# Exchanging the halves of a key tile's partitions: a permutation on TensorE and copies by ScalarE, or two DMAs

## The chip, the cores and the metric

One core of one Trainium2 chip runs the whole program. The metric is device time in microseconds (us), the median of several executions. One more execution, profiled, gives the trace.

## What is computed

Decayed causal attention over 4 batches of 8 heads (576 positions of 64 numbers), then a mixture of experts that sends each token to one of 8 experts, then a dense feed-forward layer. The change lies in the attention.

```python
scores = scale * np.matmul(q, k.transpose(0, 1, 3, 2))
decay = cum[:, :, :, None] - cum[:, :, None, :]
scores = np.where(causal, -1e9, scores + decay)
attn = np.exp(scores - max);  attn = attn / (sum(attn) + 1e-9)
attn_out = np.matmul(attn, v)
x = _moe_ref(attn_out as [2304, 512], ...)
return _moe2_ref(x, ...)
```

## The kernel before

Every number is held as two 16-bit parts, a high and a low one, so that TensorE can work in 16 bits. After the turn of queries and keys by DMA, a tile `xy[hb][:, i, 0, h]` has the high parts of a query block's 64 dimensions on partitions 0 to 63 and the low parts on 64 to 127, and `xy[hb][:, i, 1, h]` has the same of the keys. One product of the two gives high times high plus low times low. For the crossed terms the kernel needs the keys once more, with the two halves of the partitions exchanged: that is the tile `yw[hb]` (five blocks `i` of four heads, 128 columns each). `scores` (lines 568 to 608) multiplies each query block by both.

The work is cut into 8 half batches `hb` of four heads. `hb` 0 is prepared in its own way (`prep_first`, not touched). For `hb` 1 to 7, `prep_load` fetches, `prep` splits into parts, `prep_turn` (line 318) turns by DMA in three pieces, and `prep_swap` makes `yw`.

The attention is a loop over 96 units (two heads and a set of query blocks each; 12 units to a half batch, 6 to a pair of heads), as a software pipeline written out by hand: the program order is the order on every engine. Step n does `scores` of unit n+2 (TensorE), `parts_hi` of unit n-1 (ScalarE, line 671, reads `pt`), `parts_lo` of n-1 (VectorE, lines 678 and 682, reads `pt`), `maxima` of n+2 (VectorE, line 627), `values` of n-3 (TensorE, lines 713 and 727), `exps` of n+1 (ScalarE, line 650) and `turn` of n (TensorE, line 662, writes `pt`; every sixth unit writes a second tile `ptb`, line 666). Then come the side jobs that a table of numbers `PRM` gives to that step by `at(step, function)`: loads, splits, stores, routing, and in later steps parts of the first expert. The tiles `pt` and `ptb` share a pool of three PSUM slots, `ps_pt`, and a slot comes free when `parts_lo` has read it.

The half batch `hb` begins at unit 12*hb, whose scores stand in step 12*hb-2. Its swap stands in step 12*hb-6, -6, -5, -5, -6, -6 and -7 (`hb` 1 to 7; the last number of the table's rows `hb1` to `hb7`). It is two DMAs of 64 partitions each, issued by SyncE, whose queue holds all loads, turns and stores in program order.

Of the kernel before, what the change touches and what calls it, by code (L numbers as in the profile page):

```python
# [10 lines left out]
F32 = mybir.dt.float32  # L11
F16 = mybir.dt.float16
# [4 lines left out]
AF = mybir.ActivationFunctionType  # L17
# [74 lines left out]
def kernel(  # L92
# [17 lines left out]
    nc = tc.nc  # L110
# [4 lines left out]
    P = 128  # L115
    NT = 5
# [17 lines left out]
    const = ctx.enter_context(tc.tile_pool(name="const", bufs=1))  # L134
# [9 lines left out]
    identf = const.tile([P, P], F32, name="identf")  # L144
    identb = const.tile([P, P], BF16, name="identb")
    identh = const.tile([P, P], F16, name="identh")
    maskb = const.tile([P, P], BF16, name="maskb")
    mask4 = const.tile([P, 64], BF16, name="mask4")
    one3 = const.tile([P, P], BF16, name="one3")
# [34 lines left out]
    ps_pt = mid.enter_context(tc.tile_pool(name="ps_pt", bufs=3, space=PSUM))  # L184
# [66 lines left out]
    xy = {}  # L251
    yw = {}
# [93 lines left out]
            else:  # L346
                nc.vector.tensor_copy(yw[0][:, 2 * i + a, :, 0:n], tp[:, :, 0:n])

    def prep_swap(hb, part=None):

        if part in (0, None):
            yw_ = ywp.tile([P, NT, 4, P], F16, tag="yw", name="yw")
            yw[hb] = yw_
        c = (slice(0, 4), slice(4, 5), slice(0, NT))[2 if part is None else part]
        for g in range(2):
            src = slice(64 - 64 * g, 128 - 64 * g)
            dst = slice(64 * g, 64 * g + 64)
            nc.sync.dma_start(out=yw[hb][dst, c], in_=xy[hb][src, c, 1])

    def blank(hb):  # L360

# [37 lines left out]
    def identities():  # L399
        make_identity(nc, identf)  # L400
        nc.gpsimd.memset(maskb, 0.0)
        mh = maskb.rearrange("p (a c) -> p a c", a=2)
        nc.gpsimd.affine_select(
            out=mh, in_=mh, pattern=[[-1, 2], [-2, 64]], base=0, channel_multiplier=1,
            compare_op=ALU.is_ge, fill=-8.0e9,
        )

        nc.gpsimd.memset(one3, 0.0)
        nc.gpsimd.memset(one3[0:3], 1.0)
        nc.gpsimd.memset(cbt[0], 0.0)  # L410
        nc.gpsimd.memset(mask4, 0.0)
        nc.gpsimd.affine_select(
            out=mask4, in_=mask4, pattern=[[-1, 64]], base=0, channel_multiplier=1,
            compare_op=ALU.is_ge, fill=-8.0e9,
        )
# [13 lines left out]
    def cum_log():  # L429
        fs = cum["fs"]  # L430
        nc.vector.tensor_scalar(out=fs, in0=fs, scalar1=1e-4, scalar2=1.0, op0=ALU.max, op1=ALU.min)
        nc.scalar.activation(out=fs, in_=fs, func=AF.Ln)

        nc.scalar.activation(out=cum["one"][:, 0:1], in_=cum["one"][:, 0:1], func=AF.Exp, scale=0.0)
# [481 lines left out]
    def at(step, fn, *args):  # L916
        side.setdefault(max(step, -2), []).append((fn, args))
# [3 lines left out]
    for hb in range(1, 2 * B):  # L921
        o = PRM["hb" + str(hb)]
        s0 = 12 * hb
        for i in range(3):
            at(s0 + o[i], prep_load, hb, i)
            at(s0 + o[3 + i], prep, hb, i)
            at(s0 + o[6 + i], prep_turn, hb, i)
        if hb < 3:
            at(s0 + o[3], blank, hb)
        at(s0 + o[9], prep_swap, hb)  # L930
    for b in range(B):
        o = PRM["v" + str(b)]
        for t in range(NT):
# [3 lines left out]
    for gp in range(B * NPAIR):  # L937
        o = PRM["gp" + str(gp)]
# [8 lines left out]
    for b in range(B - 1):  # L947
        o = PRM["rt" + str(b)]
# [26 lines left out]
    o = PRM["tb"]  # L975
# [304 lines left out]
    o = PRM["e"]  # L1280
# [4 lines left out]
    for s in range(NE):  # L1285
        m1e, m2e = wsel(s)
        o = PRM["es" + str(s)]
# [8 lines left out]
    o = PRM["a"]  # L1296
# [15 lines left out]
    prep_load(0, 2)  # L1312
    identities()
    nc.vector.tensor_copy(identh, identf)
    nc.vector.tensor_copy(identb, identf)
    cum_log()
    prep_hi(0, 0)
# [17 lines left out]
    o = PRM["st"]  # L1335
# [228 lines left out]
    with tc.If(more > 0):  # L1564
# [3 lines left out]
        for e in range(E):  # L1568
# [7 lines left out]
            out=inb, in0=jr, in1=sx[:, :, 0:1].rearrange("p e o -> p o e").to_broadcast([P, 32, E]), op=ALU.is_ge  # L1576
        )
        nc.vector.tensor_tensor(
            out=inb2, in0=jr, in1=sx[:, :, 1:2].rearrange("p e o -> p o e").to_broadcast([P, 32, E]), op=ALU.is_ge
# [11 lines left out]
            out=ro, in0=ro, in1=sx[:, :, 0:1].rearrange("p e o -> p o e"), op=ALU.subtract  # L1591
# [19 lines left out]
        for c in (1, 2):  # L1611
            nc.vector.scalar_tensor_tensor(
                out=off[:, 0, :], in0=sel[:, c, :], scalar=noff[:, c - 1:c], in1=off[:, 0, :], op0=ALU.mult, op1=ALU.add
# [4 lines left out]
            out=inb2, in0=inb2, scalar=float(P), in1=off.to_broadcast([P, 32, E]), op0=ALU.mult, op1=ALU.add  # L1618
# [167 lines left out]
```

## Time and profile before

| | |
|---|---|
| median of 3 runs | 914.95 us (914.14 to 916.05) |
| the profiled execution | 907.73 us, of which its span is 905.6 us |
| granted TensorE clock over the span | 0.957 |
| busy: TensorE, VectorE, ScalarE, GpSimd | 88%, 56%, 35%, 32% of the span |
| attention | about 18 to 300 us of the span |
| first turn (line 662) of unit 0, of unit 95 | 24.31 us, 292.98 us |

A stretch in which every engine is partly idle is read by its waits: an engine works in program order, so whatever its next instruction waits for holds all that stands behind it. In the rows below a time at the start of a line is counted from the start of the span; a bracket at the end gives the idle time ahead of that instruction and what ended it. PE is TensorE, PEld its weight load, DVE VectorE, ACT ScalarE, POOL GpSimd, SPq the queue of SyncE.

### The profile page before, as it was taken

The numbers are of one execution on the slowest core, as the hardware profiler recorded it, in microseconds if no ns is written. First come the engines' busy times: TensorE is split into PE (matmuls) and PEld (weight loads), VectorE is DVE, ScalarE is ACT, GpSimd is POOL, SyncE is SP. The second block draws the span as 40 slices with busy tenths as digits, with TensorE's granted clock in tenths as the row PEclk, the third lists the DMA queues.
The fourth block names the chain that finished last, engine by engine and source line by source line (L and its number), as shares of the span: only waits on it lengthen the run. The fifth ranks groups of instructions, "written<-read, shape, count | busy, mean of one in ns | idle before, by whom it ended". The sixth has DMA issues, their size and how long they took to land. (4 is left out here: it accounts for less than half of the span.)

```text
span 905.6 us, 15603 instructions
## 1 busy us (share of the span) xinstructions
PE 796.8 (88%) x5565; PEld 446.1 (49%) x5565; DVE 511.5 (56%) x1244; ACT 320.6 (35%) x630; POOL 291.5 (32%) x347
## 2 busy tenths in 40 slices
PE   3987767678988885989998899999999999999995
PEld 2776656555766332434443484444444444444442
DVE  6887868686785354669788589970025015303400
ACT  4777648666665122523333122220012002101200
POOL 4443344343435224513221144350024114312400
PEclk9899998888998996999999999999999999999998
DMA  6889999989952898999999371300002000000000
GB/s 148 159 145 175 159 125 190 178 202 169 154 80 61 138 149 182 266 247 229 249 261 230 68 188 47 93 1 24 24 24 47 23 24 1 1 24 23 1 24 23
DMA packets 226631, 103.16 MB, mean 114 GB/s; under 512 B 192843, under 2 KB 213944, under 8 KB 226554
## 3 DMA queue, kind: packets, MB, share of 16 engines
q1 hardware_dynamic: 221018, 87.29, 51.5%
q0 software_dynamic: 5536, 14.86, 4.9%
q8 instruction: 46, 0.75, 0.4%
q14 instruction: 31, 0.25, 0.1%
HBM read 49.06 MB, written 15.59 MB: 71 GB/s over the span
## 5 line engine op out<-in xcount | busy, mean ns | idle before, releaser
L1675 PE MATMUL a<-x,wi 128*128 128x512 f16 x768 | 166.9, 379 | 2.7 <-DVE t L1683 2.7
L1680 DVE TENSOR_SCALAR t<-a,al 128x512 f32<-128x512 f32 (+1 forms) x80 | 55.5, 694 | 194.3 <-PE a L1675 192.7
L1675 PEld LDWEIGHTS <-wi 128*128 128x128 f16 x960 | 93.8, 98 | 99.2 <-issue 7.0
L1701 PEld LDWEIGHTS <-g 128*128 128x128 f16 x864 | 84.5, 98 | 101.9
L1691 POOL TENSOR_TENSOR g<-t,g 128x512 f16<-128x512 f32 (+1 forms) x80 | 86.2, 1078 | 111.8 <-ACT g L1690 110.1
L1231 PE MATMUL y<-wcc,ht 128*128 (+1 forms) x456 | 107.5, 391 | 12.6 <-DMA ht<-hs 12.4
L1196 PE MATMUL h<-wcc,xgt 128*128 (+1 forms) x456 | 105.6, 387 | 6.5 <-DMA xgt<-xg 6.2
L1690 ACT ACTIVATE g<-t 128x512 f16<-128x512 f32 (+1 forms) x80 | 46.7, 586 | 148.0 <-DVE t L1683 141.7
L1701 PE MATMUL o<-wo,g 128*128 128x512 f16 x432 | 96.2, 379 | 0.0
L1701 PE MATMUL o<-wob,g 128*128 128x512 f16 x432 | 96.2, 379 | 0.0
L662 PE MATMUL pt<-identf,t 128*128 128x128 f32 x384 | 66.1, 298 | 31.0 <-DVE p L678 15.4
L650 ACT ACTIVATE t<-e,nm 128x512 f32<-128x512 f32 (+2 forms) x144 | 81.3, 602 | 18.0 <-DVE e L627 12.8
L1231 PEld LDWEIGHTS <-ht 128*128 128x128 f16 x480 | 47.6, 100 | 72.1 <-DMA ht<-hs 14.6
L1196 PEld LDWEIGHTS <-xgt 128*128 128x128 f16 x480 | 47.3, 99 | 63.8 <-DMA xgt<-xg 6.8
L678 DVE SCALAR_TENSOR_TENSOR p<-pt,p 128x512 f16<-128x512 f32 x96 | 65.5, 683 | 22.3 <-ACT p L671 21.8
L1706 ACT ACTIVATE ob<-o 128x512 f32<-128x512 f32 x18 | 10.7, 597 | 169.3 <-PE o L1701 169.3
L1708 POOL DMA_INDIRECT out_dram<-ob,tka x18 | 17.6, 976 | 162.5 <-ACT ob L1706 162.5
L627 DVE TENSOR_SCALAR_CACHE_REDUCE e<-s 128x512 f32<-128x512 f32 (+3 forms) x128 | 58.1, 481 | 9.9 <-PE s L580 9.9
L662 PEld LDWEIGHTS pt<-identf,t 128*128 128x128 f32 x384 | 43.6, 149 | 35.0 <-ACT t L650 16.5
L671 ACT ACTIVATE p<-pt 128x512 f16<-128x512 f32 x96 | 56.2, 585 | 7.6 <-PE pt L662 7.3
L1683 DVE SCALAR_TENSOR_TENSOR t<-a,t 128x512 f32<-128x512 f32 (+1 forms) x80 | 51.0, 638 | 2.8
L579 PE MATMUL s<-yw,wcc 128*128 128x256 f16 (+1 forms) x192 | 47.4, 273 | 5.5 <-DMA yw<-wcc 5.5
(307 smaller groups left out, 1107.4 us busy)
## 6 DMA issues: line engine op xcount, KB each, us to landing
raw<-in_moe_w_in_dram SPq DMA_DIRECT2D x16, 512.0 KB, 6.8
raw<-in_moe_w_out_dram SPq DMA_DIRECT2D x16, 512.0 KB, 4.2
yw<-wcc SPq DMA_DIRECT2D x14, 320.0 KB, 3.9
kn<-in_k_dram SPq DMA_DIRECT2D x16, 256.0 KB, 4.7
qn<-in_q_dram SPq DMA_DIRECT2D x32, 128.0 KB, 4.3
vn<-in_v_dram SPq DMA_DIRECT2D x16, 256.0 KB, 4.1
xs<-nat SPq DMA_DIRECT2D x16, 256.0 KB, 6.9
ht<-hs SPq DMA_TRANSPOSE x40, 6.0
```

The lines of the kernel that those rows point to most:

```text
L627: nc.vector.tensor_scalar(out=e[:, c0:c0 + w], in0=ps[:, c0:c0 + w], scalar1=-1.0 / 8.0, scalar2=3.0e38, op0=ALU.mult, op1=ALU.min, accum_ ...
L650: nc.scalar.activation(out=natural(t[:, c0:c0 + w]), in_=halves(e[:, c0:c0 + w]), func=AF.Exp, scale=-1.0, bias=nm[:, y:y + 1])
L662: nc.tensor.transpose(pt[:, c * P:(c + 1) * P], e[:, c * P:(c + 1) * P], identf)
L671: nc.scalar.activation(out=p[:, 0, 0:512], in_=U[u][0], func=AF.Copy, scale=SP)
L678: nc.vector.scalar_tensor_tensor(out=p[:, 1, 0:512], in0=U[u][0], scalar=SP, in1=p[:, 0, 0:512], op0=ALU.mult, op1=ALU.subtract)
L1196: nc.tensor.matmul(hps, lhsT=xgt[:, kk, l, :], rhs=m1(m, kk, cs_), start=(kk == 0 and y == 0), stop=(kk == KD - 1 and y == 2),)
L1231: nc.tensor.matmul(yps, lhsT=ht[:, kk // (KF // 2), l, kk % (KF // 2), :], rhs=m2(m, kk), start=(kk == 0 and y == 0), stop=(kk == KF - 1 a ...
L1675: nc.tensor.matmul(hps[:, 0:n], lhsT=wi[:, mm, kk, m * P:(m + 1) * P], rhs=x2[:, l, kk, 0:n], start=(kk == 0 and y == 0), stop=(kk == KD - ...
L1680: nc.vector.tensor_scalar(out=t[:, 0:n], in0=hps[:, 0:n], scalar1=0.0, scalar2=al[:, m:m + 1], op0=ALU.min, op1=ALU.mult)
L1683: nc.vector.scalar_tensor_tensor(out=t[:, 0:n], in0=hps[:, 0:n], scalar=0.0, in1=t[:, 0:n], op0=ALU.max, op1=ALU.add)
L1691: nc.gpsimd.tensor_tensor(out=g[:, 1, 0:n], in0=t[:, 0:n], in1=g[:, 0, 0:n], op=ALU.subtract)
L1701: nc.tensor.matmul(ops, lhsT=g[:, l, t * P:(t + 1) * P], rhs=wm[:, mm, mo, :], start=(m == 0 and y == 0), stop=(m == KH - 1 and y == 2),)
```

## The change

`prep_swap` becomes five calls for each half batch, one for each block `i`. Each is a product on TensorE of a permutation matrix `other` (the identity with its two halves of columns exchanged) and the 512 columns of the block's keys, into a tile `tp` of the pool `ps_pt`, and a copy of `tp` to `yw` by ScalarE. The two DMAs on SyncE are gone. The calls stand in steps 12*hb-6 (twice), -5, -4 and -3, behind the step's `turn`; step 12*hb-6 is always the first unit of a pair of heads, and the unit before it is the one that writes `pt` and `ptb`.

```diff
+    other = const.tile([P, P], F16, name="other")
...
-    def prep_swap(hb, part=None):
+    def prep_swap(hb, i):
-        if part in (0, None):
+        if i == 0:
             yw_ = ywp.tile([P, NT, 4, P], F16, tag="yw", name="yw")
             yw[hb] = yw_
-        c = (slice(0, 4), slice(4, 5), slice(0, NT))[2 if part is None else part]
-        for g in range(2):
-            src = slice(64 - 64 * g, 128 - 64 * g)
-            dst = slice(64 * g, 64 * g + 64)
-            nc.sync.dma_start(out=yw[hb][dst, c], in_=xy[hb][src, c, 1])
+        tp = ps_pt.tile([P, 4, P], F32, tag="pt", name="tp")
+        nc.tensor.matmul(
+            tp.rearrange("p h s -> p (h s)"), lhsT=other, rhs=xy[hb][:, i, 1].rearrange("p h s -> p (h s)"),
+            start=True, stop=True,
+        )
+        nc.scalar.activation(out=yw[hb][:, i], in_=tp, func=AF.Copy)
...
-        at(s0 + o[9], prep_swap, hb)
+        for i in range(NT):
+            at(s0 + (-6, -6, -5, -4, -3)[i], prep_swap, hb, i)
...
+    nc.vector.tensor_copy(other[:, 0:64], identf[:, 64:P])
+    nc.vector.tensor_copy(other[:, 64:P], identf[:, 0:64])
```

TensorE, step 42 of the kernel after (the first swap step of half batch 4), with the semaphores that each row waits for: `pt` is the turn of unit 42, `s` the scores of unit 45 of step 43.

```order
L664 MATMUL pt<-identf,t 128x128 [waits DVE_49,Activation_49]
L664 MATMUL pt<-identf,t 128x128 x3
L356 LDWEIGHTS other [waits DMAHW6_49]
L356 MATMUL tp<-wcc,other 128x512 [waits DVE_49]
L356 LDWEIGHTS other
L356 MATMUL tp<-wcc,other 128x512 [waits DVE_49]
L577 LDWEIGHTS one_70
L577 MATMUL s<-cb_164,one_70 128x384
```

The four rows of line 356 are new, between the turn and the next step's scores. The two `tp` lie in the PSUM slots that `pt` and `ptb` of the unit before (41) had, and so wait for VectorE's reading of them; the three later `tp` of a half batch lie in slots that an earlier `tp` had, and wait for ScalarE's copy.

ScalarE, from step 18 on (half batch 2) of the kernel after: `yw<-tp` are the new copies, `v` and `wg` side jobs, `p<-pt` is `parts_hi`, `t<-e,nm` is `exps`.

```order
L360 ACTIVATE yw<-tp 128x512 x2
L388 ACTIVATE v_3_161<-vn 128x8x64
L673 ACTIVATE p<-pt 128x512
L652 ACTIVATE t<-e,nm 128x3x2x64
L652 ACTIVATE t<-e,nm 128x2x64
L360 ACTIVATE yw<-tp 128x512
L527 ACTIVATE wg_81<-wgf 128x4x8
```

The copies stand behind the step's `exps` and ahead of the next step's `parts_hi`; without them the rows are those of before.

SyncE's queue of the kernel before, around the swap of half batch 2:

```order
L788 DMA xs<-nat 128x4x256
L358 DMA yw<-wcc 64x5x512 x2
L476 DMA modi<-in_moe_modality_id_dram 128x4x2 x2
L480 DMA modi<-in_moe_modality_id_dram 64x4x2
L277 DMA kn<-in_k_dram 128x4x128
L284 DMA qn<-in_q_dram 128x4x64 x2
```

After the change the row of line 358 is missing, here and at the six other half batches, and nothing else has moved in that queue.

## Rows read from the trace of the kernel before

**Rows 1.** The page's groups: busy us, mean ns of one, idle before.

```profile
L1675 PE MATMUL a<-x,wi 128*128 128x512 f16 x768 | 166.9, 379 | 2.7 <-DVE t L1683 2.7
L671 ACT ACTIVATE p<-pt 128x512 f16<-128x512 f32 x96 | 56.2, 585 | 7.6 <-PE pt L662 7.3
```

**Rows 2.** Waits from 18 to 300 us: us in total, times, longest.

```profile
PE s L579 <- DMA yw<-wcc: 5.5, 2, 3.4
```

**Rows 3.** The page on DMA: HBM traffic; issues with KB each, us to landing.

```profile
HBM read 49.06 MB, written 15.59 MB: 71 GB/s over the span
...
yw<-wcc SPq DMA_DIRECT2D x14, 320.0 KB, 3.9
```

**Rows 4.** Half batch 1: busy time by stretch, TensorE and VectorE in time.

```profile
core 0: us, PE busy (x) PEld busy (x) DVE busy (x) ACT busy (x) POOL busy (x), PEclk, DMA share, GB/s
36.60:47.40 10.80, 8.76 (x129) 7.39 (x126) 9.82 (x29) 7.47 (x18) 4.52 (x10) 1.00 0.86 143
...
38.80 0.33 PE L575 MATMUL s<-cb,one 128*128 128x384 bf16 x1
39.13 0.27 DVE L682 SCALAR_TENSOR_TENSOR p<-ptb,p 64x128 f16<-64x128 f32 x1
47.11 0.28 PE L579 MATMUL s<-yw,wcc 128*128 128x256 f16 x1 [2.04 <-DMA yw<-wcc]
```

**Rows 5.** Half batch 2, in time: TensorE, VectorE, ScalarE, SyncE's queue.

```profile
64.53 0.33 PE L575 MATMUL s<-cb,one 128*128 128x384 bf16 x1
66.12 0.27 DVE L682 SCALAR_TENSOR_TENSOR p<-ptb,p 64x128 f16<-64x128 f32 x1
67.64 0.63 ACT L386 ACTIVATE v<-vn 128x512 f16<-128x512 f32 x1 [1.71 <-DMA vn<-in_v_dram]
70.53 1.30 SPq L358 DMA_DIRECT2D yw<-wcc  x2
75.91 1.05 SPq L284 DMA_DIRECT2D qn<-in_q_dram  x2
76.00 0.28 PE L579 MATMUL s<-yw,wcc 128*128 128x256 f16 x1 [3.42 <-DMA yw<-wcc]
80.23 0.62 ACT L258 CAST st<-qn 128x512 f16<-128x512 f32 x1 [2.07 <-DMA qn<-in_q_dram]
```

**Rows 6.** Half batch 3: busy time of its stretch, TensorE and VectorE in time.

```profile
97.60:109.30 11.70, 11.70 (x174) 10.17 (x171) 8.97 (x37) 9.24 (x22) 3.29 (x4) 0.86 0.87 170
...
98.55 0.53 PE L575 MATMUL s<-cb,one 128*128 128x384 bf16 x1
98.69 0.27 DVE L682 SCALAR_TENSOR_TENSOR p<-ptb,p 64x128 f16<-64x128 f32 x1
```

**Rows 7.** Half batch 4, in time: TensorE, ScalarE, VectorE.

```profile
129.66 0.33 PE L575 MATMUL s<-cb,one 128*128 128x384 bf16 x1
130.43 0.53 PE L713 MATMUL xp<-v,p 128*128 128x65 f16 x12
136.68 0.62 ACT L258 CAST nat<-xn 128x512 f16<-128x512 f32 x1 [9.46 <-DMA xs<-nat]
138.58 0.27 DVE L682 SCALAR_TENSOR_TENSOR p<-ptb,p 64x128 f16<-64x128 f32 x1
139.06 1.11 PE L662 MATMUL pt<-identf,t 128*128 128x128 f32 x4 [8.10 <-ACT t L650]
```

**Rows 8.** Half batch 5, in time: VectorE, TensorE.

```profile
171.73 0.27 DVE L682 SCALAR_TENSOR_TENSOR p<-ptb,p 64x128 f16<-64x128 f32 x1
171.96 1.09 PE L662 MATMUL pt<-identf,t 128*128 128x128 f32 x4 [7.58 <-DVE p L678]
```

**Rows 9.** Half batch 6, TensorE in time.

```profile
210.73 2.74 PE L1196 MATMUL h<-wcc,xgt 128*128 128x512 f16 x6 [4.38 <-DMA xgt<-xg]
```

**Rows 10.** Busy time by stretch (columns as in rows 4): two long stretches.

```profile
118.00:153.00 35.00, 23.02 (x306) 18.71 (x304) 25.28 (x81) 19.88 (x46) 16.95 (x19) 0.90 1.12 149
...
223.00:258.00 35.00, 34.86 (x429) 26.16 (x428) 28.78 (x87) 24.91 (x57) 14.83 (x18) 1.00 1.05 143
```

## Prediction

> **What bounds the kernel now.** I read the attention stage first, since the change lies in it alone, and in this order: who waits for whom, the busy time by stretch, and then the timeline around each of the seven swaps. The waits show what the two DMAs cost TensorE directly: it stood still for them twice, 5.5 us in all [rows 2]; the timeline places these at half batch 1, 2.04 us, and half batch 2, 3.42 us [rows 4, 5]. At the other five swaps `yw` was there in time. The busy time by stretch shows that no one engine sets the stage throughout: from 118 to 153 us TensorE is busy 23.02 of 35 us and the DMA share is 1.12, from 223 to 258 us TensorE is busy 34.86 of 35 [rows 10], and around half batch 1 it is VectorE with 9.82 of 10.8 us [rows 4]. So there are three kinds of place: two where the swap's DMA is waited for, two with a long stall of TensorE that another DMA began (8.10 and 7.58 us, [rows 7, 8]), and three where TensorE is busy or will be.
>
> **The change part by part.** All times are against the span of 905.6 us. Behind the attention the work is in program order on every engine, so I let a shift of its end pass to the end whole.
>
> *The price of one product.* 768 products of 512 columns kept TensorE busy 166.9 us, 0.217 each [rows 1]; 35 of them are 7.6 us where nothing hides them. After a stall they are slower: six, of the same size, took 2.74 us behind a wait of 4.38, about 0.45 each [rows 9]. *The price of one copy.* The nearest row is ScalarE's reading of a 128x512 tile out of PSUM, 0.585 us [rows 1]; 35 are 20.5 us, 2.9 for a half batch. The two small copies that build `other` run once, before the loop; I set them at nothing, at worst two VectorE rows of the 0.27 us kind [rows 4].
>
> *The wait that is added.* In a first swap step the two `tp` take the PSUM slots of the `pt` and `ptb` of the unit before, so the second waits until VectorE has read `ptb`, and behind it on TensorE stand the next step's scores, which before could go ahead. This and the copies are what has to be priced, place by place.
>
> Half batch 1: `ptb` was read at 39.13 + 0.27 = 39.40; the scores began at 38.80 [rows 4]. Held 0.6, then two products 0.43, then three 0.65: 1.7 of the 2.04 us won. ScalarE confirms how little is left: 7.47 us busy in that stretch of 10.8, with five copies 10.4 [rows 4]. I take -0.4; bounds -2.0 (all hidden) and +0.9 (the copies set the pace: 2.9 - 2.0).
>
> Half batch 2: `ptb` was read at 66.39, the scores began at 64.53 [rows 5]: held 1.9, with the two products 2.3. But ScalarE waited for a load of values until 67.64 [rows 5], so the first two copies lie in that wait; of the slip some 1.4 us are left when the place of the stall comes (2.3 + 0.65 less the 1.5 that the next steps can close while ScalarE catches up, which I judge from that 1.71 us wait). Won: 3.42 - 1.4 = 2.0. Next late is the load of queries: ScalarE met it at 80.23 after a wait of 2.07, and it was issued at 75.91, behind the swap's DMAs in the queue [rows 5]. Without these it comes earlier by 1.3 us (their issue) to 3.9 (their landing, [rows 3]), so about 2 us of the gain can pass. I take -1.9; bounds -3.4 and -0.5.
>
> Half batch 3: `ptb` was read at 98.96, the scores began at 98.55; TensorE is busy for all of 97.6 to 109.3 at a clock of 0.86 [rows 6]. Held 0.4, and five products 1.1: +1.4 rounded down a little. Bounds +0.9 (three products hidden) and +2.9 (five copies set the pace).
>
> Half batch 4: TensorE stalled to 139.06, because ScalarE waited 9.46 us for a store before it reached `parts_hi`, but ahead of that stall it had done the scores and values of step 43, from 129.66 to 130.43 + 0.53 = 130.96, 1.3 us [rows 7]. Now the two `tp` stand ahead of these and wait for `ptb`, 138.58 + 0.27 = 138.85 [rows 7]: the 1.3 us move behind the stall, with 0.43 for the pair and 0.65 for the three others, 2.4. Some idle time follows there, so I take +2.0; bounds +0.4 (only the pair) and +3.5 (the moved work and the pair at the slow rate, twice 1.73).
>
> Half batch 5 is the same picture: `ptb` read at 172.0, stall to 171.96 [rows 8]: +2.0, same bounds.
>
> Half batch 6: behind the first swap step TensorE waits for another DMA until 210.73 [rows 9], which covers the pair and its copies. Three products are left, +0.65; bounds 0 and +1.8 (three copies).
>
> Half batch 7 lies in the stretch with 34.86 of 35 us busy [rows 10]: five products, +1.1; bounds +0.5 and +2.9.
>
> *What the DMA engines get back.* 14 transfers of 320 KB go, in a stage with shares over 1 [rows 10]. After the swaps of half batches 3 to 7 I find no long wait for a transfer that stood behind them; the stalls of [rows 7, 8] began with transfers issued ahead of them. I take -0.3; bounds -4.4 (one swap's 655 KB at the 149 GB/s of [rows 10]) and 0.
>
> Sum: -0.4 - 1.9 + 1.4 + 2.0 + 2.0 + 0.65 + 1.1 - 0.3 = +4.55, so a span of about 910.1 us. The profiled execution took 907.73 us, 2.1 beside its span and 7.2 less than the median of the runs, 914.95; I add the sum to that median: **919.5 us**.
>
> **The rivals.** *Hidden:* products and copies fall into idle time, as ScalarE's 19.88 busy of 35 us [rows 10] would allow, and only the two stalls go: 914.95 - 5.46 = 909.5 us, faster. It decides itself at half batches 4 and 5: if the moved 1.3 us find idle time behind the stall and TensorE is not held at half batches 1 to 3. Against it: at each of these `ptb` is read after the scores could start.
>
> *DMA sets the pace:* where the share is over 1, time follows bytes. Five swaps, 3.28 MB at 149 GB/s, are 22 us; less 7.6 of products: about 900 us. Against it: TensorE and VectorE are near full in parts of that stretch, and the long stalls are single late transfers. The Trainium skill (Perfetto Trace Analysis, Identifying the Most-Contended Engine) says to work on the most occupied engine first, which by the share would be the DMA engines; the same place says that for DMA the HBM utilisation is to be read instead, as occupancy of 16 engines misleads. The page of the profile has 71 GB/s [rows 3], and the swaps move nothing in HBM, so by the second half of the rule this rival weakens.
>
> *No difference:* the added 8 us at half batches 3 to 7 are swallowed, since the long waits are for transfers that land when they land: 915 us.
>
> *ScalarE sets the pace:* all 35 copies lie on the path: 20.5 - 5.5 = +15, 930 us.
>
> **How the numbers follow.** A measurement of this kernel can tell 0.2%, 1.8 us, from no change. Forecast (slower by 2 to 9 us) 0.56; ScalarE 0.05; no difference 0.17; hidden 0.15; DMA 0.07. So faster 0.22, same 0.17, slower 0.61. The bounds of the terms add up to -7.6 and +15, but not all can be at one end. The range, 908 to 926, holds the forecast, no difference and most of hidden, and leaves out DMA, ScalarE and the ends, 0.2. The likeliest one's own range is 917 to 924.
>
> **What would show it.** In the profile after: no row of TensorE waiting for `yw`; waits of `tp` for VectorE of about 8 us at half batches 4 and 5 in place of those of [rows 7, 8], with the scores of step 43 behind them; ScalarE busier by 20 us or a little less; the last turn later by about 4 us. Wrong it is if these scores run at no cost, or if the waits for stores and loads shrink in the stretch from 118 to 223 us.

## The result, and the profile after

The kernel after is slower: 921.6 us (median of 11 runs, 917.54 to 924.02) against 913.1 for the kernel before in the same runs, a ratio of 1.0117, interval 1.0092 to 1.0143. In a second set of runs it was 927.08 against 919.25, ratio 1.0079, interval 1.0046 to 1.0113. The ratios leave out runs that lie more than 1.5% above the fastest of their kernel and are not the quotient of the two medians, so where they tell different things both are given: by the medians 8.5 and 7.8 us were added, by the ratios 10.7 and 7.3, where 4.55 had been forecast. The sign was right, 921.6 lies in the range, and the size came out about twice as large. The intervals are 0.25 to 0.35% to either side, wider than the 0.2% that the prediction thought could be told from no change. The median of the kernel before differs between sets (913.1 to 920.4), so every kernel below is compared with the runs of before of its own set.

The first lines of the profile of after, from its page: the groups that answer to [rows 1], HBM traffic as in [rows 3], and the DMA queue (packets, MB, share).

```profile
L1680 PE MATMUL a<-x,wi 128*128 128x512 f16 x768 | 166.9, 379 | 2.6 <-DVE t L1688 2.6
...
L673 ACT ACTIVATE p<-pt 128x512 f16<-128x512 f32 x96 | 56.6, 590 | 4.1 <-PE s L582 3.5
...
q1 hardware_dynamic: 216314, 82.70, 48.9%
...
HBM read 49.06 MB, written 15.59 MB: 70 GB/s over the span
```

The groups of ScalarE from 18 to 315 us, and the products of line 356 (duration in ns, least, median, most):

```profile
L360 ACT ACTIVATE yw<-tp 128x512 f16<-128x512 f32 x35 | 20.0, 593 | 13.1 <-PE tp L356 13.0
...
L356 PE MATMUL tp<-wcc,other x35: 376/379/634, 38.6 to 266.5; 128*128 128x512 f16 x35
```

35 copies keep ScalarE busy for 20.0 us, as forecast from [rows 1] (20.5). The 4.6 MB of the swaps are gone from the queue, which had 87.29 MB before, while HBM traffic stands where it stood. The waits of the attention, the longest that have to do with the change (us in total, times, longest):

```profile
PE tp L356 <- DVE p L680: 25.5, 3, 14.9
...
ACT nat L259 <- DMA xs<-nat: 16.8, 2, 14.2
```

No row of TensorE waiting for `yw` is left; in its place TensorE waits 25.5 us, in three places, with a `tp` for VectorE. They are half batch 2 (1.67), 4 (14.95) and 5 (8.87). In time, the kernel after at half batches 1 and 2 (compare [rows 4, 5]):

```profile
38.35 0.27 DVE L684 SCALAR_TENSOR_TENSOR p<-ptb,p 64x128 f16<-64x128 f32 x1
38.57 0.59 PE L356 MATMUL tp<-wcc,other 128*128 128x512 f16 x2
39.00 0.33 PE L577 MATMUL s<-cb,one 128*128 128x384 bf16 x1
...
64.64 0.27 DVE L684 SCALAR_TENSOR_TENSOR p<-ptb,p 64x128 f16<-64x128 f32 x1
64.77 0.59 PE L356 MATMUL tp<-wcc,other 128*128 128x512 f16 x2 [1.67 <-DVE p L680]
65.20 0.32 PE L577 MATMUL s<-cb,one 128*128 128x384 bf16 x1
```

At half batch 1 `ptb` was read as TensorE came to the pair, so nothing was held; at half batch 2 the pair waited 1.67 us and the scores behind it with it. Half batch 4, where most was lost (compare [rows 7]): ScalarE, VectorE, TensorE.

```profile
142.51 0.62 ACT L259 CAST nat<-xn 128x512 f16<-128x512 f32 x1 [14.22 <-DMA xs<-nat]
144.41 0.27 DVE L684 SCALAR_TENSOR_TENSOR p<-ptb,p 64x128 f16<-64x128 f32 x1
144.55 1.01 PE L356 MATMUL tp<-wcc,other 128*128 128x512 f16 x2 [14.95 <-DVE p L680]
145.35 0.53 PE L577 MATMUL s<-cb,one 128*128 128x384 bf16 x1
147.52 1.01 PE L664 MATMUL pt<-identf,t 128*128 128x128 f32 x4
```

The pair and the scores of step 43 stand behind the stall, as forecast; from ScalarE's cast to the turn of unit 43 are 5.01 us, where [rows 7] have 2.38 (136.68 to 139.06). But the stall itself ended 5.8 us later than in [rows 7] (the cast at 142.51, not 136.68). Half batches 5 and 6 in time (compare [rows 8, 9]), and busy time by stretch (columns as in [rows 4]; first the stretch of half batch 3, and last the second of [rows 10], read 16 us later):

```profile
179.40 1.01 PE L356 MATMUL tp<-wcc,other 128*128 128x512 f16 x2 [8.87 <-DVE p L680]
182.37 0.66 PE L664 MATMUL pt<-identf,t 128*128 128x128 f32 x4
...
221.45 2.74 PE L1199 MATMUL h<-wcc,xgt 128*128 128x512 f16 x6 [4.07 <-DMA xgt<-xg]
```

```profile
94.45:106.94 12.49, 12.49 (x180) 10.05 (x178) 8.04 (x35) 11.18 (x25) 3.32 (x4) 0.89 0.58 89
118.00:153.00 35.00, 15.60 (x181) 12.49 (x180) 16.18 (x64) 14.43 (x34) 11.49 (x13) 0.71 1.14 101
239.00:274.00 35.00, 34.69 (x423) 25.44 (x420) 27.46 (x90) 26.00 (x59) 13.18 (x18) 1.00 0.61 101
```

From 118 to 153 us TensorE is busy 15.60 us instead of 23.02. The DMA engines moved 101 GB/s there instead of 149 at nearly the same share, 1.14 and 1.12; only one of the seven swaps, 0.66 MB, lay in that stretch, so the rest of what is missing, about 1 MB, is other transfers that no longer fall into it. At half batch 3 and in the last stretch TensorE is busy nearly throughout, as before.

### The profile page after: what moved, and what is told of

Read it like the earlier page. It is cut to its first block, busy times and chain, and to the rows that moved or that the text cites. A ratio compares the mean times of both kernels' runs of the same rounds, so it can differ in the third digit from the quotient of the medians.

```text
span 921.0 us, 15708 instructions
## 1 busy us (share of the span) xinstructions
PE 804.4 (87%) x5600; PEld 449.4 (49%) x5600; DVE 509.5 (55%) x1246; ACT 337.8 (37%) x665; POOL 292.3 (32%) x347
## 5 line engine op out<-in xcount | busy, mean ns | idle before, releaser
L1234 PE MATMUL y<-wcc,ht 128*128 (+1 forms) x456 | 105.8, 387 | 11.0 <-DMA ht<-hs 10.7
L1234 PEld LDWEIGHTS <-ht 128*128 128x128 f16 x480 | 47.1, 99 | 70.2 <-DMA ht<-hs 15.1
L1711 ACT ACTIVATE ob<-o 128x512 f32<-128x512 f32 x18 | 10.7, 597 | 169.3 <-PE o L1706 169.3
L580 PE MATMUL s<-wcc 128*128 128x256 f16 (+1 forms) x192 | 49.3, 272 | 0.6 <-issue 0.6
```

The source lines that it names most:

```text
L1234: nc.tensor.matmul(yps, lhsT=ht[:, kk // (KF // 2), l, kk % (KF // 2), :], rhs=m2(m, kk), start=(kk == 0 and y == 0), stop=(kk == KF - 1 a ...
```

## The experiments

**Do the two kernels repeat?** Both were profiled once more, unchanged.

> The kernel before, unchanged, for a second profiled execution. The kernel after took 921.6 us against 913.1, but its profiled span is 15.4 us longer; 5.8 of that arose where ScalarE waits for a store of normalised rows (9.46 us before, 14.22 after), a transfer issued ahead of the swap. Theory A (that wait wanders from execution to execution, and the swap's own cost is the rest): a second trace of before shows this wait 2 us or more away from 9.46, with the turns of units 36 and 54 moved by as much. Theory B (the wait is lengthened by the change): here it is within 1 us of 9.46.

> The kernel after, unchanged, for a second profiled execution and times beside the other kernels of this set. Theory A (the store's wait at half batch 4 wanders): its wait differs from 14.22 us by 2 us or more, and what the swap itself adds at half batches 3 to 7 (the turn of each unit against the one before) repeats within 0.5 us: +1.8, +1.5, +1.9, about +3 and +1.1, with -1.1 and -2.9 at half batches 1 and 2. Theory B (the change lengthens the wait): 13 us or more again. Time 921.6, within 3 us.

In time, the issue of the store that ScalarE waits for, in both traces of before and then in both of after, and ScalarE's cast in the second trace of before and in that of after:

```profile
124.67 0.59 SPq L788 DMA_DIRECT2D xs<-nat  x1
125.41 0.59 SPq L788 DMA_DIRECT2D xs<-nat  x1
124.30 0.58 SPq L790 DMA_DIRECT2D xs<-nat  x1
124.36 0.58 SPq L790 DMA_DIRECT2D xs<-nat  x1
```

```profile
138.74 0.62 ACT L258 CAST nat<-xn 128x512 f16<-128x512 f32 x1 [7.24 <-DMA xs<-nat]
```

```profile
140.37 0.62 ACT L259 CAST nat<-xn 128x512 f16<-128x512 f32 x1 [10.98 <-DMA xs<-nat]
```

The wait wanders: 9.46 and 7.24 us before, 14.22 and 10.98 after. It moves by 2.2 and 3.2 us between executions of one kernel, which is theory A's condition in both runs and not theory B's; but it is longer in both traces of after, which theory A doesn't say. From the store's issue to the cast are 12.0 and 13.3 us before, 18.2 and 16.0 after. The time of after, 927.08, is not within 3 us of 921.6, in a set in which before is slower as well; the second execution of before took 920.85. The starts of some turns (line 662 or 664) in the four traces tell where the time goes; the last columns are the difference of the mean durations, after less before, and the forecast:

```
                    before  before again   after  after again
turn of unit 6       38.33     38.11       38.10     38.08
             17      61.92     59.73       60.43     61.18
             28      90.20     88.54       85.81     86.61
             36     113.50    111.40      111.10    111.11
             54     162.59    164.17      169.87    168.75
             62     194.34    197.92      203.91    203.63
             77     239.52    248.26      252.47    255.50
             85     263.56    272.30      277.59    280.61
             95     292.98    305.47      308.86    311.96

units    half batch   measured   forecast
 6 to 17     1          +0.1       -0.4
17 to 28     2          -3.1       -1.9
28 to 36     3          +1.8       +1.4
36 to 54     4          +7.3       +2.0
54 to 62     5          +1.7       +2.0
62 to 77     6          +2.5       +0.65
77 to 85     7          +1.1       +1.1
85 to 95     -           0.0
```

The two traces of before differ by 3.7 us from unit 36 to 54 and by 5.2 from 62 to 77, those of after by 1.1 and 3.3, so only half batch 4 lies above its forecast by clearly more than that. Half batch 2, where two traces of one kernel agree within 0.6, did 1.2 us better than forecast.

**What do the parts cost?** The swap left out altogether, and the products without the copies.

```diff
-    def prep_swap(hb, part=None):
...
+    def prep_swap(hb, i):
+        yw[hb] = yw[0]
```

> Leaves the exchange of the key halves out for half batches 1 to 7 (the crossed products read half batch 0's tile instead): neither DMAs, products nor copies. Theory A (the change pays by the held PSUM slots, the moved work and the copies, and the DMAs cost only their two stalls): 5 to 7 us below before, 906 to 909, and 13 to 15 below after. Theory B (without the swap's DMAs SyncE's queue runs ahead and the transfers behind collide, which lengthens the store's wait at half batch 4): the wait is 13 us or more here too, though no product or copy is there, and the time is no more than 3 us below before.

```diff
         if i == 0:
-            yw_ = ywp.tile([P, NT, 4, P], F16, tag="yw", name="yw")
-            yw[hb] = yw_
+            yw[hb] = yw[0]
...
-        nc.scalar.activation(out=yw[hb][:, i], in_=tp, func=AF.Copy)
```

> The kernel after without its 35 copies on ScalarE; the crossed products read half batch 0's tile. The products into the shared PSUM slots stand where they stood. Theory A (the pair of products holds TensorE until VectorE has read the slots, and the moved scores follow): within 3 us of after, 918 to 921, since nearly all of the cost is the hold. Theory C (ScalarE's copies are what is paid): 6 to 10 us below after, 911 to 915.

No swap: 913.6 against 919.25, ratio 0.9932 (0.9901 to 0.9962), 6.2 us by the ratio (3.5 to 9.1), 5.7 by the medians: about the two stalls of [rows 2]. In the second trace of before only the one at half batch 2 is there (3.51 us). So the DMAs of the kernel before cost about what their waits show; that their bytes ran beside other transfers cost no more than the interval allows. Products alone: 921.87, ratio 1.0040 (1.0009 to 1.0071). From the medians, products and held slots cost 8.3 us (921.87 less 913.6) and the copies 5.2 more (927.08 less 921.87), from the ratios 9.9 and 3.6. That lies between theory A, which gave the copies 3 at most, and theory C, which gave them 6 to 10; with intervals of 3 us to either side neither is excluded, but the larger part is not the copies. In time, the cast at half batch 4 in the two, no swap first:

```profile
136.46 0.62 ACT L258 CAST nat<-xn 128x512 f16<-128x512 f32 x1 [9.32 <-DMA xs<-nat]
```

```profile
138.20 0.62 ACT L259 CAST nat<-xn 128x512 f16<-128x512 f32 x1 [11.62 <-DMA xs<-nat]
```

The store that they wait for was issued at 121.33 and 121.53, so it took 15.1 and 16.7 us until the cast; in after it took 18.2 and 16.0, in before 12.0 and 13.3.

**Does SyncE's queue run ahead?** In before, SyncE had issued the loads of queries by 128.54 and stood at the swap of half batch 4 until 133.73, when the turned keys had landed; the loads and stores behind it stood too.

```diff
+    def swap_gate(hb):
+        nc.sync.dma_start(out=gate[:, hb], in_=xy[hb][0:8, :, 1, 0, 0:8])
...
+        at(s0 + o[9], swap_gate, hb)
```

> The kernel after, and one small DMA (8 partitions, 40 numbers each, into a tile that nobody reads) at the place of each swap's DMAs in SyncE's queue. It waits for the turned keys as they did, and so holds the loads and stores behind it, but moves next to nothing. Theory B (without that wait the transfers behind run ahead and share the slow stretch with the store that ScalarE waits for at half batch 4): from the store's issue to ScalarE's cast 12 to 13.5 us as with the DMAs (12.0 and 13.3 in two traces), not 16.0 to 18.2 as after; the time 3 to 5 us below after, about +3 to +5 against before. Theory A (the products and copies alone, and chance): the store takes 15.5 us or more and the time is within 2 us of after, +6 to +10.

In time, SyncE's queue and then ScalarE's cast in this kernel:

```profile
124.26 0.59 SPq L794 DMA_DIRECT2D xs<-nat  x1
136.88 0.84 SPq L364 DMA_DIRECT2D gate<-wcc  x1
138.56 0.61 SPq L794 DMA_DIRECT2D xs<-nat  x1
```

```profile
139.72 0.62 ACT L260 CAST nat<-xn 128x512 f16<-128x512 f32 x1 [10.43 <-DMA xs<-nat]
```

The gate held the next store to 138.56 (132.80 in after), and still the store of 124.26 took 15.5 us. 926.82 against 919.28, ratio 1.0072 (1.0045 to 1.0099), as after. Theory B's 12 to 13.5 us and its 3 to 5 below after are not met.

**Does the pair hold the scores behind it?** The calls moved ahead of the turn, behind the step's scores and values.

```diff
-            at(s0 + (-6, -6, -5, -4, -3)[i], prep_swap, hb, i)
+            ahead.setdefault(s0 + (-5, -5, -4, -3, -3)[i], []).append((prep_swap, (hb, i)))
...
+        for fn, args in ahead.get(n, []):
+            fn(*args)
         if 0 <= n < TOT:
             turn(n)
```

> The kernel after, with the five products and copies moved ahead of the turns of steps -5, -5, -4, -3, -3 (before: behind the turns of steps -6, -6, -5, -4, -3), so that the scores and values of the step stand ahead of the pair. Theory A (the held pair delays the scores behind it): 1.3 us less at half batches 4 and 5 each, 0.6, 1 and 0.4 at half batches 1 to 3: 3 to 5 us below after. Rival (the turn behind the pair needs the same slots, so the wait only moves): within 1.5 us of after.

918.91 against 919.28, ratio 0.9979 (0.9944 to 1.0015): the whole loss is gone by the times, 8 us below after (927.08, in a set with the same median of before) and below the kernel with the gate (926.82, in this set), where 3 to 5 were expected. Half batch 4 in time, ScalarE and then TensorE:

```profile
139.97 0.62 ACT L259 CAST nat<-xn 128x512 f16<-128x512 f32 x1 [8.01 <-DMA xs<-nat]
```

```profile
142.00 1.01 PE L356 MATMUL tp<-wcc,other 128*128 128x512 f16 x2 [6.92 <-DVE p L680]
144.19 1.12 PE L664 MATMUL pt<-identf,t 128*128 128x128 f32 x4 [1.17 <-DVE p L680]
```

From the cast to the turn are 4.22 us instead of 5.01, and the store (issued at 126.44) took 13.5. From unit 36 to 54 this trace took 52.9 us, 5 to 6 less than after (58.8 and 57.6); but it had come to unit 36 4.4 us later (115.47), for from unit 17 to 28 it took 28.0 us, as before and not as after (25.4). Its last turn is at 310.70, no earlier than after's 308.86 and 311.96, and it is shorter only behind the attention. So the time shows that the place of the pair matters, and the trace doesn't show where the 8 us come from.

**Which half batches pay?** DMAs and products mixed by half batch.

```diff
-        for i in range(NT):
-            at(s0 + (-6, -6, -5, -4, -3)[i], prep_swap, hb, i)
+        if hb in (1, 2):
+            for i in range(NT):
+                at(s0 + (-6, -6, -5, -4, -3)[i], prep_swap, hb, i)
+        else:
+            at(s0 + o[9], swap_dma, hb)
```

> The products and copies for half batches 1 and 2 only, the two DMAs for 3 to 7. By the turns of each unit, the two places win 0.5 to 1.1 and 2.9 us. Theory A (each place pays by itself): 3.4 to 4 us below before. Rival (a later wait for a load or store takes the gain back): within 1.5 us of before.

The next has `(3, 4, 5, 6, 7)` in that line:

> The DMAs for half batches 1 and 2, the products and copies for 3 to 7. Theory A (each place pays by itself): after's difference without the two gains, 11 to 13 us above before. Rival (what is lost at 3 to 7 is set by transfers that land when they land): 7 to 9, the same as after.

1 and 2: 917.42 against 919.28, ratio 0.9975 (0.9943 to 1.0008), -2.3 us, between the two expectations and what the prediction had for these two (-2.3). 3 to 7: 923.48, ratio 1.0028 (0.9993 to 1.0063), +2.6 (by the medians +4.2), below both. The two add up to +0.3 (by the medians +2.3), and after has +7 to +11: the places do not simply add. From unit 36 to 54 the kernel with products at 3 to 7 took 54.1 us, after 58.8 and 57.6, before 49.1 and 52.8. Its store took 13.2, though the products of half batch 4 are in it: these alone do not make the store land late.

**Is half batch 4 the place?** Products at 1, 2, 3, 5, 6 and 7, the DMAs back at 4 alone:

```diff
+        if hb in (1, 2, 3, 5, 6, 7):
```

> The kernel after with the two DMAs back at half batch 4 alone. Theory D (the mis-sized term is half batch 4, where TensorE's stall ends with the store that ScalarE waits for and the moved work stands behind it; 5.4 us in the traces): 4.5 to 6.5 us below after, +2 to +5 against before; ScalarE's cast to unit 43's turn takes 2.4 us, not 5.0. Rival F (the excess is spread over all places, or lies in the copies): 0 to 2 below after, +6 to +10 against before.

920.62 against 918.62, ratio 1.0030 (1.0007 to 1.0053), +2.8 us (by the medians +2.0): in the span of theory D, below F's. In time, ScalarE's cast, and the turn of unit 43:

```profile
138.61 0.62 ACT L259 CAST nat<-xn 128x512 f16<-128x512 f32 x1 [12.56 <-DMA xs<-nat]
```

```profile
140.99 1.12 PE L675 MATMUL pt<-identf,t 128*128 128x128 f32 x4 [11.21 <-ACT t L663]
```

From cast to turn 2.38 us again, as in before. The store took 15.1 here, with the DMAs at half batch 4: by this trace these are not what made it land earlier in before.

**What if ScalarE needn't wait for that store?** A third buffer for the tile of normalised rows, in before and in after.

```diff
-        nat = xnp.tile([P, 4, 2, 2, D], F16, tag="nat", name="nat")
+        nat = xnp.tile([P, 4, 2, 2, D], F16, tag="nat", name="nat", bufs=3)
```

> The kernel before with a third buffer for the tile of normalised rows (nat), so that ScalarE's cast at half batch 4 need not wait for the store of two tiles ago (9.46 and 7.24 us in two traces). Both theories: that wait is gone and the stall of TensorE at unit 43 falls from 8.1 us to 3 or less; 4 to 7 us below before, if no later wait takes it back.

> The kernel after with the same third buffer. Over the traces so far the change costs 5.4 us at half batch 4, of which 1.8 (2.6 less what closes behind) is the moved work and 3.6 a later landing of the store. Theory D (that landing is the mis-sized term): without the wait for it the change costs 4 to 6 us, so 4 to 6 above the third buffer's kernel before. Rival E (the products at half batch 4 now wait for the turned keys, which SyncE saw landed at 133.7 and 134.1 us, 4 to 5 us behind the turn of unit 42): TensorE waits there for a transfer instead, and the change costs 8 us or more still.

The kernel before with it: 919.43 against 920.42, ratio 0.9989 (0.9959 to 1.0020). The kernel after with it: 917.86, ratio 0.9988 (0.9963 to 1.0012). The change, which cost 7 to 11 us, costs nothing that these runs can tell (the ratios are equal, the medians 1.6 apart the other way), less than theory D's 4 to 6 and far from E. The traces say why. Before with the third buffer in time, ScalarE's cast, then TensorE at units 43 and 48:

```profile
129.86 0.60 ACT L258 CAST nat<-xn 128x512 f16<-128x512 f32 x1
```

```profile
132.81 0.63 PE L662 MATMUL pt<-identf,t 128*128 128x128 f32 x4
...
145.07 0.39 PE L579 MATMUL s<-yw,wcc 128*128 128x256 f16 x1 [6.15 <-DMA yw<-wcc]
```

After with the third buffer, the same places (the pair of step 42 and the turn of unit 43):

```profile
126.11 0.61 ACT L259 CAST nat<-xn 128x512 f16<-128x512 f32 x1
```

```profile
128.83 0.59 PE L356 MATMUL tp<-wcc,other 128*128 128x512 f16 x2 [0.49 <-DVE p L680]
131.41 0.66 PE L664 MATMUL pt<-identf,t 128*128 128x128 f32 x4 [0.85 <-ACT yw L360]
```

The stall at unit 43 is gone in both. With the DMAs the next thing late is `yw`: issued at 136.55, it is waited for 6.15 us, and most of the gain is returned. With the products `yw` is on the spot, the pair waits 0.49 us, and the gain is kept. From unit 36 to 54 these two took 48.6 and 46.6 us, where before took 49.1 and 52.8 and after 58.8 and 57.6. So the third buffer gives the kernel after about 12 us there and the kernel before about 2, and that the two now come out alike has two parts: the long wait is gone from the one, and the other has a new one for `yw`.

**A better version.** The third buffer, with products at half batch 2 alone, where before lost most:

```diff
+        if hb in (2,):
...
+        nat = xnp.tile([P, 4, 2, 2, D], F16, tag="nat", name="nat", bufs=3)
```

> The third buffer, and the products and copies for half batch 2 alone, the one place where the traces show a gain of nearly 3 us; the DMAs for the others. Theory A (each place pays by itself): 2.5 to 3 us below the third buffer's kernel before, 7 to 10 below before. Rival (a later wait takes it back, as at half batches 1 and 2 together, 1.9 where 3.4 to 4 was expected): within 1.5 us of the third buffer's kernel before.

913.49 against 920.42, ratio 0.9957 (0.9930 to 0.9985): below both kernels, by 0.4% of before, 3.9 us. Against the third buffer's kernel before it is 2.9 us by the ratios, as theory A has it, and 5.9 by the medians (919.43); the 7 to 10 below before are not reached. Its trace still waits for the DMA's `yw` at half batch 4:

```profile
139.67 0.27 PE L592 MATMUL s<-yw,wcc 128*128 128x256 f16 x1 [3.62 <-DMA yw<-wcc]
```

## Why the prediction was right and where it was wrong

*The time.* Forecast were 919.5 us, 914.95 and 4.55, and 921.6 were measured. That these are so close is in part luck: before had 913.1 in the same runs, so the change itself was 8.5 us or more.

*What bounds the kernel.* Right: the two waits for `yw` of [rows 2], 5.46 us, are nearly all that the DMAs cost; without any swap 6.2 us are saved. The term for the DMA engines, -0.3, stands with that. The rival in which DMA sets the pace is out: without the swaps' 4.6 MB, and with no product in their place, 6.2 us were saved and not the 22 that it had put down. The Trainium skill's rule that weakened it (Perfetto Trace Analysis, Identifying the Most-Contended Engine: for DMA the HBM utilisation, not occupancy) agrees with the traces: a share of 1.14 after as of 1.12 before, at 101 and 149 GB/s.

*Half batches 1 and 2.* The kernel with products there alone gave -2.3, the forecast's -0.4 and -1.9. The traces divide it otherwise: nothing at 1, where the hold was nothing and 0.61 us (forecast 0.6) in the two traces of after and the wait for the DMA was absent in before's second trace, and -3.1 at 2, where the hold of 1.67 (forecast 1.9) was closed sooner than I had allowed.

*Half batches 3, 5, 6 and 7.* +1.8, +1.7, +2.5 and +1.1 against +1.4, +2.0, +0.65 and +1.1. Together with 1 and 2 the kernel with the DMAs at 4 alone gives +2.8, and the forecast without its term for 4 was +2.55. So these six terms stand as a sum, as far as an interval of +0.6 to +4.9 shows it; 6 was too small, within what traces of one kernel differ by.

*Half batch 4.* This is the step that failed, a term of the sum that was mis-sized. I priced the work that moves behind the stall at +2.0, with bounds +0.4 and +3.5, and took the stall's end as given, since its transfer was among those "issued ahead of them". The moved work was right: from ScalarE's cast to the turn of unit 43 are 5.0 us in the traces with the pair there (5.01 after and 5.01 again, and in products alone 5.01) and 2.4 with the DMAs or without a swap, 2.6 in the step, of which up to 1.3 closes behind it (0.4 on the mean of the four traces). By the ratios, after in its two sets less the kernel with the DMAs back at 4, the place cost 4.5 to 8 us; by the four traces 7.3. The rest is the end of the stall, later by 2 to 6 us, because the store took 16 to 18 us from its issue and not 12 to 13; the prediction had put a later end at nothing. That the loss hangs on this wait is borne out by the third buffer: without the wait the change goes from +7 to +11 down to nothing, in part because the DMAs then have a wait of their own at the same place. The last turn, forecast about 4 us later, came 11 us later by the means of the two traces each.

*What stays open* is why the store lands later. It isn't that transfers behind it are let go sooner (the gate), nor the missing DMAs of half batch 4 (15.1 us with them back). Of eleven traces that have this wait, the three with the DMAs at half batch 3 show 11.7 to 13.3 us, and the eight without show 13.2 to 18.2; no run tests that alone, and one trace each is little. Nor is the products' presence at half batch 4 enough: with them the store took 13.2 (products at 3 to 7) and 13.5 (calls ahead of the turn) as well as 18.2. So that the change itself makes the store land late is not shown. Why the calls ahead of the turn recover all 8 us, when their step at half batch 4 shrinks by 0.8 and the trace wins nothing up to the last turn, is open too.

*Rivals.* "Hidden" decided itself as it was put down: at half batches 4 and 5 TensorE was held, at half batch 2 as well. "ScalarE sets the pace" at +15 was too strong, but the copies may not be free: 3.6 to 5.2 us by the times, where I had let them vanish beside the products.

## What to carry to other kernels

Seven transfers of which two are waited for cost about those two waits. Replacing them pays at most where they were waited for (here at half batch 2, not clearly at 1), so change the one or two places and leave the others. Before work is put behind a long stall, take the stall's own cause away: here one more buffer turned a loss of 1% into nothing, and with the products at one place came out 0.4% below before. A wait that ends with a transfer is no constant: take a second trace before its end is used as a term of a sum.

## What the hardware showed

The store that takes so long lies in a stretch where the DMA engines show a busy share over 1 and move little. Busy time by stretch in before, then in after, columns as in [rows 4]:

```profile
110.00:124.00 14.00, 11.32 (x143) 9.43 (x142) 12.84 (x47) 10.33 (x25) 6.95 (x9) 0.88 1.28 173
124.00:135.00 11.00, 4.60 (x70) 3.83 (x67) 5.55 (x14) 2.74 (x5) 5.00 (x5) 1.00 1.14 54
```

```profile
110.00:124.00 14.00, 9.78 (x134) 7.95 (x134) 11.48 (x44) 8.57 (x21) 6.74 (x8) 1.00 1.37 170
124.00:141.00 17.00, 3.14 (x31) 2.77 (x32) 3.75 (x9) 2.81 (x6) 4.39 (x4) 0.61 1.31 34
```

The share is 1.14 and 1.31, the rate falls from over 170 to 54 and 34 GB/s, and the slow stretch is 11 us in the one and 17 in the other. It begins as GpSimd issues the last of five scatters of single numbers into HBM (the profile's list of DMA issues from 118 to 128 us in before, median us to landing last):

```profile
ids<-tokid,posi POOLq DMA_INDIRECT x5, 9.8
```

The Trainium skill (DMA: Bandwidth & Descriptors, Specifications) gives 512 bytes as the least transfer for full rate, below which the engines read, modify and write. The scatters' 4-byte numbers lie far below that, but no run here shows that it is they that slow the transfers behind them. SyncE's queue has stores of single numbers too, two of them at 122.18 and 122.77 us, just ahead of the store of 124.67; and in before a share of 1.33 at 69 GB/s also stands from 175 to 180 us, 13 us before GpSimd's next scatter.

Behind the last turn the program is the same in all kernels of this study but for its start, and yet took from 606.0 us (calls ahead of the turn) to 620.8 (the third buffer in before) in the traces, 611.7 to 613.5 in both kernels and with no swap. A span of one trace is therefore no measure of a change of a few us. The turns inside the stage, from two traces of each kernel, and medians of ten runs tell more, within the differences shown above.
